# Three scatters of a second table moved between those of a first one, on GpSimd's queue

## The chip, the core and the metric

The kernel runs on one core of one Trainium2 chip, in one launch. The metric is the device time of one execution in microseconds (us); the median of several runs counts. The engines are named as in the profile: PE is TensorE (PEld is its loading of weights), DVE is VectorE, ACT is ScalarE, POOL is GpSimd and SP is SyncE. SP only starts transfers. Each engine works through its own queue in program order.

## What is computed

Three stages follow each other, for 1536 tokens of 512 features. A block-wise linear attention gives x; a dense layer follows; then a mixture of eight experts, in which each expert takes exactly 192 tokens:

```
x = attention(q, k, v, lam)                 # 1536 x 512
h = x @ w_in;  x2 = (h * clip(h + 3, 0, 6) / 6) @ w_out
logits = x2 @ w_gate                        # 8 experts
order = argsort(-logits.flatten())          # best (token, expert) pairs first
for idx in order:                           # a token goes to an expert that is not full
    tok, e = divmod(idx, 8)
    if assigned[tok] < 0 and counts[e] < 192: assigned[tok] = e; counts[e] += 1
for e in range(8):
    out[assigned == e] = relu(x2[assigned == e] @ w1[e]) @ w2[e]
```

## The kernel before

**Chunks and tables.** The tokens lie in 12 chunks of 128, numbered j from 0 to 11. The dense layer's second product gives x2 (PE, line 647, tile `x2p`). For chunks 0 to 7 one product gives all 512 features of a chunk; for chunks 8 to 11 it gives 384, and the last 128 features of these four chunks come at the very end from one product of their own (`x2_rest`, line 682, tile `x2q`), which is copied by ACT (`xq`), transposed on PE (line 691, tile `x2t`) and written by ACT and DVE (lines 694 and 695) into tile `xb`. Each value is held as two 16-bit parts, a high and a low one. So every token has a row of 768 entries in tile `xa` (384 features, two parts) and one of 288 in `xb` (128 features, two parts, and its number).

**Scatters.** While x2 is being computed, DVE, POOL and PE find the assignment in seven phases. At its end DVE writes `pos` (line 865): the place of each token in a table sorted by expert. Then POOL scatters the rows into two tables in device memory: twelve indirect transfers (one per chunk, j = 0 to 11) from `xa` into table `xsa`, here called a0 to a11, and twelve from `xb` into `xsb`, here called b0 to b11. Function `scatter` (line 875) puts a memset of one column, tile `spare`, ahead of each of them, and declares that scatters to the same table do not depend on each other.

**Experts.** The experts go in pairs. For each pair SP reads the 384 rows of the pair back with a transposing transfer: entries 0 to 767 of `xsa` (line 897) into the first six slices of tile `xs`, entries 0 to 255 of `xsb` (line 898) into the last two. Then SP loads the tokens' numbers (lines 903 and 904) and the weights (line 975). The first layer (`layer1`, line 922, tile `hp`) has four units for each expert, and each unit has two steps: one of 18 products that needs only the part from `xsa`, and one of 6 products that needs the part from `xsb` too. ACT turns a finished unit into `rr` (line 928), DVE into the two parts of `h` (lines 408 and 416), and the second layer (line 952, tile `po`) reads `h`. Its results go out by twelve more scatters.

**The order of the work.** A planner in the kernel writes out the order of each engine's queue before anything runs. Every step has booked costs, steps that it waits for and a key; among the steps that could start at the same moment on an engine the one with the smallest key comes first. A transfer is booked to end so (t is its start, the lines are 150 and 151):

```
self.dma = max(self.dma, t + 1.3) + s.nbytes * 2.78e-6
s.end = self.dma + 0.9
```

The steps named in the planner only fix the order; on the chip an instruction waits only for the data and the buffers that it really uses. In the first layer of experts 0 and 1 the 18-product steps have keys 0, 2, 4, 6 (expert 0) and 9, 11, 13, 15 (expert 1), counted from the same start, and the 6-product steps 10, 12, 14, 16 and 19, 21, 23, 25. The keys of the scatters are `GK + j` for a and `GK + 12 + j` for b.

Of the kernel before, what the change touches and what calls it, by code (L numbers as in the profile page):

```python
# [15 lines left out]
P = 128  # L16
NCH = 12
# [10 lines left out]
XB = 288  # L28
# [20 lines left out]
class Plan:  # L49
# [16 lines left out]
    def buf(self, pool, shape, dt, name):  # L66
        return Buf(self, pool, shape, dt, name)

    def add(self, eng, cost=0.0, fn=None, deps=(), bufs=(), key=0.0, reserve=0, nbytes=0):
        ways = {eng: (cost, fn)} if fn else eng  # L70
        s = Step(ways, [d for d in deps if d is not None], list(bufs), key, reserve, nbytes)
        for b in s.bufs:
            b.left += 1
        self.steps.append(s)
        return s
# [117 lines left out]
def fused_kernel(ctx, tc, raw_d, lam_d, win_d, wout_d, wg_d, w1_d, w2_d, out):  # L193
    nc = tc.nc
    te, ve, se, ge, sy = nc.tensor, nc.vector, nc.scalar, nc.gpsimd, nc.sync
# [21 lines left out]
    def C(shape, dt, name):  # L217
        return cst.tile(shape, dt, name=name)
# [411 lines left out]
    GK = -1e6  # L630

    xab, t_xa, t_xb = {}, [None] * NCH, [None] * NCH
    x_key = unit_key[4, 15] + 3
    JB = 8
    ids_in = []
    xbb = buf("B", [P, NCH, XB], F16, "xb")
# [229 lines left out]
    t_pos = add("ve", 0.9, slots, [t], [rk], GK)  # L866
# [5 lines left out]
    xsb_d = dram.tile([NCH * P, XB], F16, name="xsb")  # L872
    spare = C([P, 1], F32, "spare")

    def scatter(dst, idx, src, done):
        ge.memset(spare, 0.0)
        s = ge.indirect_dma_start(out=dst, out_offset=bass.IndirectOffsetOnAxis(ap=idx, axis=0), in_=src, in_offset=None)  # L877
        for o in done:
            tc.declare_no_dep(s.ins, o.ins, reason="distinct rows")
        done.append(s)  # L880
    sca, scb = [], []
    t_sa = [add("ge", 1.28, lambda j=j: scatter(xsa_d[:, :], pos[:, j:j + 1], xab[j // 4][:, j % 4], sca),
                [t_pos] + t_xa[j], [xab[j // 4]], GK + j, 0, 2 * P * XA) for j in range(NCH)]
    t_sb = [add("ge", 1.28, lambda j=j: scatter(xsb_d[:, :], pos[:, j:j + 1], xbb[:, j], scb),
                [t_pos] + t_xb[j] + ids_in, [xbb], GK + NCH + j, 0, 2 * P * XB) for j in range(NCH)]


    rows = C([P, NE // 2, 3], I32, "rows")
# [45 lines left out]
    def put(ps, q, z, t, key):  # L934
        os = buf("Q", [P, 512], F32, f"os{q}_{z}")
        t = add("se", c_se(512), lambda: se.activation(os[:], ps[:], AF.Copy, scale=2.0 ** -23), t, [ps, os], key)
        add("ge", 1.1, lambda: scatter(out, rows[:, q, z:z + 1], os[:], oscat), [t, t_rows], [os], key, 0, 262144)
# [104 lines left out]
```

## Time and profile before

| what | value |
|---|---|
| median of 3 runs | 514.68 us (512.02 to 515.46) |
| time of the profiled execution | 515.91 us |
| its span, first to last instruction | 514.0 us |
| mean granted PE clock | 0.986 of full |
| PE busy | 485.0 us (94%) |
| DVE busy | 397.8 us (77%) |
| ACT busy | 309.0 us (60%) |
| POOL busy | 166.6 us (32%) |

The span is what the trace covers; the 1.9 us between it and the time of that execution lie around it. Busy times are sums over the whole span; what one stage is worth is read from that stage.

### The profile page before, as it was taken

To read this page: it belongs to the slowest core of one execution; us is meant where nothing else is said; L and a number is where in the kernel's file an instruction comes from. 1 tells how busy PE (TensorE), PEld (TensorE's weight loads), DVE (VectorE), ACT (ScalarE), POOL (GpSimd) and SP (SyncE) were. 2 spreads that over 40 slices of the span, in tenths; PEclk is the share of its full clock that TensorE was granted. 3 is DMA by queue.
4 is the path that set the end of the run, shared out by engine and by line. 5 is a ranking of instruction groups with operands and counts; after the bars stand their busy time and mean duration, and the time that the engine had idled before them with its cause. 6 is when DMAs were issued, how large, how long until landed. Compare 5 with 4: busy or idle time off the path is not lost.

```text
span 514.0 us, 10307 instructions
## 1 busy us (share of the span) xinstructions
PE 485.0 (94%) x4241; PEld 296.7 (58%) x4243; DVE 397.8 (77%) x707; ACT 309.0 (60%) x486; POOL 166.6 (32%) x174
## 2 busy tenths in 40 slices
PE   7687998999999999999999999999969999999995
PEld 3476444688785444534434443556459676776762
DVE  7689999988688877589899889877524878889620
ACT  1476959764556664377669558745423767687510
POOL 2013343120222220167347436618860312223211
PEclk9889999999999999999999999999979999999999
DMA  7999326220264550000000000667368999995011
GB/s 224 400 416 412 148 83 246 84 42 2 83 246 91 97 94 8 2 1 1 1 1 2 1 1 7 240 246 240 132 149 261 327 400 356 360 354 215 1 42 41
DMA packets 44910, 77.86 MB, mean 151 GB/s; under 512 B 33080, under 2 KB 34112, under 8 KB 38720
## 3 DMA queue, kind: packets, MB, share of 16 engines
q1 hardware_dynamic: 42752, 70.82, 41.0%
q0 software_dynamic: 2112, 6.39, 3.3%
q8 instruction: 33, 0.54, 0.4%
q14 instruction: 13, 0.11, 0.1%
HBM read 63.46 MB, written 6.40 MB: 136 GB/s over the span
## 4 chain that ended last, share of the span: by engine, by line
DVE 38%; issue 22%; PE 18%; POOL 8%; ACT 8%; DMA 5%; POOLq 0%; SPq 0%; DVEq 0%; ACTq 0%
PE x2p L647 9%; DVE G L809 7%; DVE r L536 4%; DVE G L800 3%; DVE g L416 3%; POOL w L410 3%; POOL out L877 2%; ACT kd L439 2%; DVE sm L458 2%; ACT g L406 2%; DVE eq L782 2%; PE h L221 2%; DVE wid L391 2%; PE cp L828 2%; PE h L223 2%
## 5 line engine op out<-in xcount | busy, mean ns | idle before, releaser
L647 PE MATMUL x2p<-wo,g 128*128 128x512 f16 (+1 forms) x576 | 124.6, 362 | 0.0
L221 PE MATMUL h<-xT,wi 128*128 128x256 f16 (+2 forms) x304 | 90.8, 306 | 2.8 <-DVE r L536 2.8
L222 PE MATMUL h<-xT,wi 128*128 128x256 f16 (+2 forms) x304 | 90.7, 306 | 0.0
L223 PE MATMUL h<-xT,wi 128*128 128x256 f16 (+2 forms) x304 | 90.6, 306 | 0.0
L647 PEld LDWEIGHTS <-g 128*128 128x128 f16 x576 | 52.5, 99 | 55.6 <-issue 10.5
L775 POOL TENSOR_SCALAR eq<-mrow,m 128x128 bf16<-128x128 f32 x56 | 56.7, 1030 | 84.6 <-DVE on L748 52.1
L416 DVE SCALAR_TENSOR_TENSOR w<-ws,w 128x1024 f16<-128x1024 f32 x58 | 71.4, 1276 | 5.8 <-ACT w L406 5.8
L922 PE MATMUL hp<-xs,w 128*128 128x192 f16 x768 | 67.4, 251 | 3.8 <-DMA xs<-xsa 3.8
L922 PEld LDWEIGHTS <-w 128*128 128x128 f16 x768 | 65.1, 100 | 7.6 <-issue 5.2
L952 PE MATMUL po<-w,h 128*64 128x512 f16 (+1 forms) x384 | 64.1, 380 | 0.1
L406 ACT ACTIVATE w<-ws 128x1024 f16<-128x1024 f32 x64 | 63.9, 1048 | 0.1
L809 DVE TENSOR_SCALAR G<-mrow,m 128x1408 bf16<-128x1408 f32 (+10 forms) x77 | 52.0, 706 | 0.0
L385 POOL TENSOR_SCALAR wod<-wod 128x1024 f32<-128x1024 f32 x8 | 22.5, 2818 | 89.3 <-ACT wod L383 75.5
L406 ACT ACTIVATE g<-r 128x512 f16<-128x512 f32 (+1 forms) x52 | 30.8, 595 | 30.5 <-DVE r L536 29.6
L952 PEld LDWEIGHTS <-h 128*64 128x64 f16 (+1 forms) x384 | 29.0, 104 | 31.8 <-issue 1.7
L416 DVE SCALAR_TENSOR_TENSOR g<-r,g 128x512 f16<-128x512 f32 (+1 forms) x52 | 34.3, 662 | 11.4 <-ACT g L406 11.0
L536 DVE SCALAR_TENSOR_TENSOR r<-r,h 128x512 f32<-128x512 f32 (+1 forms) x52 | 33.1, 639 | 10.1 <-ACT r L535 9.8
L535 ACT ACTIVATE r<-h,c 128x512 f32<-128x512 f32 (+1 forms) x52 | 33.4, 644 | 10.9 <-PE h L223 10.8
L803 ACT ACTIVATE G<-mrow,m 128x1536 bf16<-128x1536 f32 (+3 forms) x28 | 39.4, 1407 | 0.8
L222 PEld LDWEIGHTS <-wi 128*128 128x128 f16 x304 | 30.6, 101 | 15.9 <-issue 3.2
L928 ACT ACTIVATE rr<-hp 128x384 f32<-128x384 f32 x32 | 15.6, 490 | 40.0 <-PE hp L922 39.8
L221 PEld LDWEIGHTS <-wi 128*128 128x128 f16 x304 | 30.5, 100 | 15.0 <-issue 1.5
(154 smaller groups left out, 693.2 us busy)
## 6 DMA issues: line engine op xcount, KB each, us to landing
ws<-w SPq DMA_DIRECT2D x32, 1024.0 KB, 9.3
raw<-raw SPq DMA_DIRECT2D x24, 512.0 KB, 10.0
wis<-w_in SPq DMA_DIRECT2D x8, 1024.0 KB, 14.1
wos<-w_out SPq DMA_DIRECT2D x8, 1024.0 KB, 7.8
tab<-tz SPq DMA_DIRECT2D x1, 512.0 KB, 6.3
wt<-wo SPq DMA_TRANSPOSE x16, 3.2
xsa<-xa,pos POOLq DMA_INDIRECT x12, 4.9
xsb<-xb,pos POOLq DMA_INDIRECT x12, 2.7
```

Of the source, the lines that this page charges most:

```text
L221: te.matmul(ps, lh, rh, start=start, stop=False)
L222: te.matmul(ps, lh, rl, start=False, stop=False)
L223: te.matmul(ps, ll, rh, start=False, stop=stop)
L406: h = add("se", c_se(n), lambda: se.activation(dst()[0], src(), AF.Copy, scale=sc), deps, bufs, key, reserve)
L416: lo = add("ve", c_ve(n), lambda: ve.scalar_tensor_tensor(dst()[1], src(), sc, dst()[0], op0=OP.mult, op1=OP.subtract), [h], bufs, key)
L536: t = add("ve", c_ve(nf * T), lambda: ve.scalar_tensor_tensor(r[:], r[:], 6.0 * 2.0 ** -11, ps[:], op0=OP.min, op1=OP.mult), [t], [ps, r], ...
L647: te.matmul(ps[:], gsl(y, fc, j), w[:, z, fc % 4, d0:d1], start=(fc + y + z == 0), stop=(fc == 15 and y == 1))
L775: t_eq.append(add("ge", 1.06, lambda i=i, eq=eqs[0], mrow=mrow: ge.tensor_scalar(eq[:, i], mrow[:, P * i:P * i + P], m[:, i:i + 1], None, ...
L803: se.activation(G[:, z, 0:o], mrow[:, 0:o], AF.Sign, scale=-1.0, bias=m[:, i:i + 1])
L809: ve.tensor_scalar(G[:, z, o:], mrow[:, o:], m[:, i:i + 1], None, op0=OP.is_le)
L922: te.matmul(ps[:, i], w[:, z, kk % 2, cl], x[:, 2 * kk + y, CAP * i0:CAP * i0 + CAP], start=(i + kk + y + z == 0), stop=(i == 1 and kk == ...
L952: te.matmul(o, h1[e][:, y, k, cl], w2[e, fh][0][:, zz, f], start=(k + y + zz == 0), stop=(k == 7 and y == 1))
```

## The change

A list `last_to` remembers which table the scatter before went to, and the memset is put ahead of a scatter only if that was the same table. The scatters b0, b1 and b2 get keys that put them behind a2, a5 and a8 and name these as steps to wait for in the planner; b3 to b11 name a11. The scatters of the results use the same function, so the first of them loses its memset as well.

```
+    last_to = []
+
     def scatter(dst, idx, src, done):
-        ge.memset(spare, 0.0)
+        if last_to[-1:] == [id(done)]:
+            ge.memset(spare, 0.0)
+        last_to.append(id(done))
...
     t_sb = [add("ge", 1.28, lambda j=j: scatter(xsb_d[:, :], pos[:, j:j + 1], xbb[:, j], scb),
-                [t_pos] + t_xb[j] + ids_in, [xbb], GK + NCH + j, 0, 2 * P * XB) for j in range(NCH)]
+                [t_pos] + t_xb[j] + ids_in + ([t_sa[3 * j + 2]] if j < 3 else t_sa[-1:]), [xbb], GK + (3 * j + 2.5 if j < 3 else NCH + j), 0, 2 * P * XB)
+            for j in range(NCH)]
```

## Rows read from the trace of the kernel before

**Rows 1.** PE's part of the timeline: start, us, line, operation, tile, count.

```profile
373.77 0.65 PE L691 MATMUL x2t<-ident,xq 128*128 128x128 f32 x4 [0.69 <-ACT xq L686]
378.26 18.37 PE L922 MATMUL hp<-xs,w 128*128 128x192 f16 x192 [3.84 <-DMA xs<-xsa]
396.77 10.52 PE L952 MATMUL po<-w,h 128*128 128x512 f16 x48
407.13 4.12 PE L922 MATMUL hp<-xs,w 128*128 128x192 f16 x48
...
420.67 8.09 PE L922 MATMUL hp<-xs,w 128*128 128x192 f16 x96
...
492.27 15.82 PE L952 MATMUL po<-w,h 128*128 128x512 f16 x96
```

**Rows 2.** Single microseconds: busy by engine, then granted PE clock, DMA share, GB/s.

```profile
376.00:377.00 1.00, 0.00 (x0) 0.00 (x0) 0.96 (x1) 0.95 (x2) 0.82 (x1) 0.68 1.20 328
...
382.00:383.00 1.00, 1.00 (x8) 0.92 (x7) 0.00 (x0) 0.00 (x0) 0.00 (x0) 0.50 0.21 74
...
384.00:385.00 1.00, 1.00 (x16) 1.00 (x13) 0.00 (x0) 0.00 (x0) 0.00 (x0) 1.00 0.32 50
```

**Rows 3.** SP's part of the timeline, from the first transposing transfer on.

```profile
372.47 5.84 SPq L897 DMA_TRANSPOSE xs<-xsa  x2
383.20 1.21 SPq L898 DMA_TRANSPOSE xs<-xsb  x1
...
388.01 1.50 SPq L975 DMA_DIRECT2D ws<-w  x3
```

**Rows 4.** POOL's part of the timeline: some of the 24 scatters and a memset.

```profile
346.56 1.92 POOL L877 DMA_INDIRECT xsa<-xa,pos  x1 [11.10 <-DVE pos L865]
348.49 0.12 POOL L876 MEMSET spare<- 128x1 f32 x1
348.78 0.96 POOL L877 DMA_INDIRECT xsa<-xa,pos  x1 [0.18 <-issue]
...
366.59 1.96 POOL L877 DMA_INDIRECT xsb<-xb,pos  x1 [0.19 <-issue]
...
368.86 1.97 POOL L877 DMA_INDIRECT xsa<-xa,pos  x1 [0.19 <-DVE w L416]
...
374.92 0.96 POOL L877 DMA_INDIRECT xsb<-xb,pos  x1 [0.19 <-issue]
...
376.18 1.91 POOL L877 DMA_INDIRECT xsb<-xb,pos  x1 [0.19 <-issue]
...
380.91 0.96 POOL L877 DMA_INDIRECT xsb<-xb,pos  x1 [0.19 <-issue]
```

**Rows 5.** DVE's part of the timeline.

```profile
363.28 0.56 DVE L662 SCALAR_TENSOR_TENSOR xa<-x2p,xa 128x384 f16<-128x384 f32 x1 [4.50 <-ACT xa L661]
364.23 6.90 DVE L416 SCALAR_TENSOR_TENSOR w<-ws,w 128x1024 f16<-128x1024 f32 x6 [0.39 <-ACT w L406]
...
375.09 0.69 DVE L695 TENSOR_TENSOR xb<-x2t,xb 128x512 f16<-128x512 f32 x1 [3.96 <-ACT xb L694]
376.04 2.36 DVE L416 SCALAR_TENSOR_TENSOR w<-ws,w 128x1024 f16<-128x1024 f32 x2 [0.25 <-ACT w L406]
...
392.24 0.36 DVE L408 TENSOR_SCALAR h<-rr 128x384 f16<-128x384 f32 x1 [13.84 <-ACT rr L928]
...
393.11 0.35 DVE L408 TENSOR_SCALAR h<-rr 128x384 f16<-128x384 f32 x1
```

**Rows 6.** Landing time of the first transfer of line 898, issued at 383.2 us.

```profile
DMA to landing us min/median/max: 4.9/4.9/4.9
```

**Rows 7.** Landing times of the scatters, the window 345 to 383 us.

```profile
DMA to landing us min/median/max: 2.3/3.6/7.4
```

**Rows 8.** ACT's part of the timeline: the first layer's units.

```profile
391.72 1.48 ACT L928 ACTIVATE rr<-hp 128x384 f32<-128x384 f32 x3 [14.77 <-PE hp L922]
394.69 2.47 ACT L928 ACTIVATE rr<-hp 128x384 f32<-128x384 f32 x5 [1.49 <-PE hp L922]
```

## Prediction

> **What bounds the kernel now.** I read the busy shares first, then PE's timeline, then the wait at its one gap, and from there back along SP, POOL and DVE. PE is what the whole span hangs on (485.0 of 514.0 us busy), so an edit to POOL's queue pays only where PE waits for it. While the scatters begin, PE still computes x2 without a break. It ends that work with the last transposes at 373.77 + 0.65 = 374.42, then stands still for 3.84 us until the first rows read back from the first table land, at 378.26 [rows 1]. From there to the last product, 492.27 + 15.82 = 508.09, its timeline has no further gap. What PE saves between 374.4 and 396.8 can thus be carried to the end.
>
> The gap has a price behind it as well. The granted clock falls to 0.50 of full in it (2.4 to 1.2 GHz), stays there until 383 and is 1.00 from 384 [rows 2]. A first-layer block at full clock takes 8.09 us for 96 products, 0.0843 us each; the 192 after the gap took 18.37 us where two such blocks take 16.18. So 2.2 us were lost to the clock.
>
> The wait goes back like this. The first transposing transfer starts at 372.47 and lands 5.79 us later, when PE starts [rows 1, 3]. It waited for the last scatter of the first table, a11, which POOL began at 368.86: 3.61 us from there to the transfer, 1.97 of them its own issue [rows 3, 4]. The rows that a11 sends were ready at 363.28 + 0.56 = 363.84 [rows 5]. So a11 lost 5 us in POOL's queue, where four scatters of the second table stood ahead of it. The second transfer, from the second table, starts at 383.20, lands 4.9 us later, at 388.1 [rows 3, 6], and waited for b11 (begun 380.91). b8 to b11 send rows that DVE writes at 375.09 to 375.78 [rows 5], and b8 began at 376.18, just behind.
>
> **Fewer scatters ahead of a11.** After the change eleven a and three b stand ahead of it, fourteen where it had fifteen. The fifteenth scatter began at 366.59 (b3) [rows 4], so that is when a11 would begin if nothing else changed: 2.27 us earlier, and behind its data.
>
> **Memsets left out.** Three b between the a make six places ahead of a11 where the table changes and the memset goes; a seventh is between a11 and b3. (The very first memset, and that of the first result scatter, run while POOL waits for others: nothing.) The one removed takes 0.12 us, and then 0.19 us pass before the scatter [rows 4]. A bare scatter is in no row. Its price lies between a gain of 0.31 (memset and pause both go) and a loss, x, which I bound by the landing: if a bare scatter waited for the one before it to land, at 2.3 to 7.4 us [rows 7] where 1.27 pass now, x would be 1.0 to 6.1 us. The nearest row is the memset itself: I take 0.12 to 0.31 saved, since scatters already follow each other at 1.27 us without waiting for a landing. Six times that is 0.7 to 1.9 us. So a11 begins at 364.7 to 365.9, say 365.3, the transfer at 368.9, and PE can start at 374.7, practically as soon as it is free. The gap of 3.84 us shrinks to 0.3, and with it goes the reason for the slow clock.
>
> The Trainium skill, GPSIMD Engine Reference, section Instruction dispatch, says that consecutive Pool instructions don't wait for each other's completion; a core starts the next when its share is done. By that x is zero and the change can't lose on POOL; no row here shows a bare pair.
>
> **What is late next.** b3 to b7 follow a11: from 365.3 + 1.97, with five at 1.27 us and one long one, they end at about 374.8, before the rows of b8 are ready. b8 therefore still begins at about 376.1, b11 and its transfer stay where they were, and the second table lands at 388.0 rather than 388.1. Of the 192 first-layer products of experts 0 and 1, 144 need only the first table: 144 x 0.0843 = 12.1 us, from 374.7 to 386.8. Then PE waits 1.2 us for the second table, a new gap. The remaining 48 take 4.05 us: 392.05, where they now end at 396.63.
>
> This needs the planner to put all eight 18-product steps ahead of the first 6-product step. Before it did not: ACT's three units in a row, a wait of 1.49 us, then five [rows 8] fit seven long steps, three short, the eighth long (18 x 0.0843 = 1.52 us), five short, which is the order of the keys once the second table is booked. Afterwards b3 waits, in the plan, for a11's booked landing, at X. By the bookings in the code (two latencies, the 1.3 and 0.9 us of a transfer, 725,000 bytes) the long steps are then ready at X + 0.16 + 1.3 + 2.02 + 0.9 + 0.56 = X + 4.9, while b3 starts at X + 0.16, b11 eight times 1.28 later at X + 10.4, lands at X + 12.8, and its transfer, with 2.87 and latencies of 0.16 and 0.56, makes the short steps ready at X + 16.4 or later. The distance of 11.4 us is more than seven long steps (booked at 10.4), so the eighth goes ahead. On the chip b3 does not wait for a11: the tables are distinct. These bookings give only the order; no time is taken from them.
>
> **The second layer.** It needs all of expert 0's h. Before, DVE began on the first unit at 392.24, 0.7 us after that unit's products ended, and took 0.87 us for each unit [rows 5]. Now the first unit ends at 388.5, DVE begins at 389.2, has four by 392.65, and PE goes on at 392.85, after 0.8 us more of idleness. Before it went on at 396.77: **3.9 us gained**. Expert 2's products come 10.4 us later, at 403.3 (407.13 now). The loads for its weights start at 388.01 [rows 3], still behind the transfer of line 898, so they come no earlier; before, their last needed split ended near 404, behind DVE's h work, which now ends 3.5 us sooner, and ACT's and DVE's splits of the landed weights can end near 401.4. That covers it by 2 us, and the later weights are loaded into buffers that PE itself frees, so they shift with it.
>
> **Sum.** The span goes from 514.0 to 510.1, the profiled time from 515.91 to 512.0. The median shown is 1.23 below the profiled time, so it goes from 514.68 to **510.8 us**. This hardly hangs on the memsets: PE starting 1.2 us later would only fill its wait for the second table.
>
> **Rivals.**
> First, the order on PE stays at seven long steps (chance 0.1). Then PE waits from 385.3 to 388.0 and has 66 products left: it goes on at about 393.5, 3.2 us gained, or, if the clock falls in that gap, 2.2 less: 511.5 to 513.7. For it: the planner's other bookings could shift the second table; against it, the distance above comes from one chain of steps.
> Second, the clock falls in the new gap at 387 (0.1). Before, the mean of 0.68 in the microsecond from 376 [rows 2] is full speed up to 376.36 and half after it, so PE had done nothing for 1.9 us when it fell; 1.2 is under that. If it falls, 2.2 us go: 512.8.
> Third, the weights of experts 2 and 3 become late and eat part of the shift (0.1): against it the 2 us above, for it that DVE, which makes half of each split, is busy 77% of the span. 1.5 to 2.5 us gained: about 512.7.
> Fourth, slower: a bare scatter waits for the one before it. With x each, a11 moves by 6x and b8 to b11 by 7x less the 0.9 us by which b7 now ends before b8 needs the queue. The second table then sets the end, and the change turns into a loss from 7x - 0.9 = 3.9, x = 0.7 us. At x = 1.3 (landing 2.6) the loss is 4.3: 519.0; at 6.1 it would be 37.9, some 552. Against it: spaced scatters never wait for a landing, and a memset of 0.12 us is little to make that difference; for it: nothing else says why a memset of an unused column stood there. 0.1.
> That the change doesn't reach the chip (b0 to b2 are planned behind a11 after all) makes a11 earlier still and changes nothing in the sum, since the second table decides.
> In the forecast itself (0.6) one variant matters. Five of the 24 scatters took 1.9 to 2.0 us instead of 0.96, b8 among them, beside DVE's two products at 376.04 [rows 4, 5]. Were b8 short, the end would come 1 us sooner, 509.8. The Trainium skill, GPSIMD Engine Reference, section Specifications, says that POOL shares its SBUF interfaces with VectorE and contends with instructions that have two SBUF inputs; those of line 416 are such, and b3, a11 and b8 agree. By it b8 stays long, as it is released by the same DVE work.
>
> **How the numbers follow.** The likeliest case gives 510.8, with its variant and a spread of runs of about 1 us 508.8 to 511.8; the first three rivals reach to 514. So 508.8 to 514.2, leaving out the fourth and a little beside. About 1% (5.1 us) is what a measurement of this kernel can tell from no change. Faster by more needs 509.5 or less, the variant with a favourable median: 0.18. Slower by over 1%: most of the fourth rival, 0.08. The rest, 0.74, within.
>
> **What would show it.** In the changed profile: a11 begun at 365 to 366; the first transfer at about 369; the first layer beginning by 375, at full clock; PE's timeline with a wait of about 1 us before 388 whose releaser is the second table; eight units of `rr` in one run; the second layer from about 393. Wrong it would be if bare scatters stand over 1.3 us apart, if the transfer from the second table starts later than 383.2, if the clock falls at 387, or if PE waits for weights near 403.

## The result and the profile after

The changed kernel takes 508.68 us (median of 11 runs, 507.6 to 511.18) where the one before takes 514.68: a ratio of 0.9893, 95% interval 0.987 to 0.9916. By the ratio that is 5.5 us (509.2), by the medians 6.0. The median lies 0.1 us under the range of the prediction and 2.1 under its number; the 509.2 us of the ratio lie inside the range. Of the three chances the one for faster by over 1%, 0.18, is the one that came about by a hair: 1.07%, with an interval that reaches to either side of 1%.

The profiled execution has a span of 506.3 us. It had reached the first scatter, a0, 1.9 us sooner than the one before (344.67 against 346.56 [rows 4]), ahead of all that the change touches, and the last transposes as much sooner (371.88 against 373.77 [rows 1]); that part is not the change's. The changed kernel run again had the transposes at 371.08, the same order with all memsets at 374.48: this differs from execution to execution. I therefore count from the start of the transposes. PE's timeline, columns as in [rows 1]:

```profile
371.88 0.66 PE L691 MATMUL x2t<-ident,xq 128*128 128x128 f32 x4 [0.69 <-ACT xq L686]
372.38 12.04 PE L928 MATMUL hp<-xs,w 128*128 128x192 f16 x144
384.74 4.12 PE L928 MATMUL hp<-xs,w 128*128 128x192 f16 x48 [0.32 <-DMA xs<-xsb]
389.01 10.52 PE L958 MATMUL po<-w,h 128*128 128x512 f16 x48
...
484.51 15.82 PE L958 MATMUL po<-w,h 128*128 128x512 f16 x96
```

The gap of 3.84 us is gone. All 144 products that need only the first table run at once (12.04 us); then PE waits 0.32 us, and the releaser is now the second table. From the transposes to the second layer it takes 17.13 us, where it took 396.77 - 373.77 = 23.00: 5.87 us. From there to the end of the span it is 117.3 us in both (506.3 - 389.01 and 514.0 - 396.77), so in this pair of traces the whole of it arrives.

SP's timeline, which answers to [rows 3]; the transfer from the second table is line 904 (898 before):

```profile
366.05 5.39 SPq L903 DMA_TRANSPOSE xs<-xsa  x2
381.71 1.21 SPq L904 DMA_TRANSPOSE xs<-xsb  x1
```

The instructions of that line with their landing, as in [rows 6]:

```profile
L904 SPq DMA_TRANSPOSE xs<-xsb x1: 1214/1214/1214, 381.7 to 381.7; - x1
...
DMA to landing us min/median/max: 3.0/3.0/3.0
```

POOL's timeline ([rows 4] before), from a5 on:

```profile
352.96 0.96 POOL L881 DMA_INDIRECT xsa<-xa,pos  x1 [0.19 <-issue]
354.22 0.96 POOL L881 DMA_INDIRECT xsb<-xb,pos  x1 [0.30 <-issue]
355.49 1.11 POOL L881 DMA_INDIRECT xsa<-xa,pos  x1 [0.30 <-issue]
356.60 0.12 POOL L879 MEMSET spare<- 128x1 f32 x1
356.90 0.96 POOL L881 DMA_INDIRECT xsa<-xa,pos  x1 [0.19 <-issue]
...
359.43 0.96 POOL L881 DMA_INDIRECT xsb<-xb,pos  x1 [0.30 <-issue]
360.69 0.96 POOL L881 DMA_INDIRECT xsa<-xa,pos  x1 [0.30 <-issue]
...
363.23 1.17 POOL L881 DMA_INDIRECT xsa<-xa,pos  x1 [0.19 <-issue]
364.71 1.96 POOL L881 DMA_INDIRECT xsb<-xb,pos  x1 [0.30 <-issue]
...
375.17 1.43 POOL L881 DMA_INDIRECT xsb<-xb,pos  x1 [0.19 <-issue]
...
379.43 0.96 POOL L881 DMA_INDIRECT xsb<-xb,pos  x1 [0.19 <-issue]
```

The pauses tell the two kinds apart. Ahead of a bare scatter there are 0.30 us; with a memset there are 0.12 of memset and 0.19 of pause. Either way the next scatter begins 1.26 to 1.27 us after one of 0.96. The planner put only b0 and b1 ahead of a11, behind a5 (354.22) and a8 (359.43); b2 follows a11 (364.71). Clock, ACT and DVE (columns as in [rows 2], [rows 8], [rows 5]):

```profile
376.00:377.00 1.00, 1.00 (x16) 1.00 (x14) 0.00 (x0) 0.00 (x0) 0.81 (x3) 1.00 0.08 16
...
384.00:385.00 1.00, 0.68 (x10) 0.53 (x8) 0.00 (x0) 0.00 (x0) 0.00 (x0) 1.00 0.35 20
```

```profile
385.44 3.96 ACT L934 ACTIVATE rr<-hp 128x384 f32<-128x384 f32 x8 [11.23 <-PE hp L928]
```

```profile
373.95 0.68 DVE L695 TENSOR_TENSOR xb<-x2t,xb 128x512 f16<-128x512 f32 x1
...
385.96 0.36 DVE L408 TENSOR_SCALAR h<-rr 128x384 f16<-128x384 f32 x1 [10.19 <-ACT rr L934]
...
388.94 0.56 DVE L416 SCALAR_TENSOR_TENSOR h<-rr,h 128x384 f16<-128x384 f32 x1
```

The clock stays at 1.00 through the first layer. The eight units leave PE in one run. The fourth unit of `h` ends at 388.94 + 0.56 = 389.50, half a microsecond after PE has gone on with the second layer.

### The profile page after: what moved, and what is told of

The parts are those of the page before. It is cut to its first block, busy times and chain, and to the rows that moved or that the text cites. A ratio compares the mean times of both kernels' runs of the same rounds, so it can differ in the third digit from the quotient of the medians.

```text
span 506.3 us, 10304 instructions
## 1 busy us (share of the span) xinstructions
PE 484.0 (96%) x4241; PEld 294.2 (58%) x4243; DVE 398.6 (79%) x707; ACT 309.1 (61%) x486; POOL 166.4 (33%) x167
## 4 chain that ended last, share of the span: by engine, by line
PE 35%; DVE 35%; issue 9%; ACT 8%; DMA 7%; POOL 5%; POOLq 0%; SPq 0%; DVEq 0%; ACTq 0%
PE x2p L647 11%; DVE G L809 7%; PE hp L928 6%; PE po L958 6%; DVE G L800 3%; DVE r L536 3%; DMA ws<-w 3%; DVE g L416 3%; POOL xsb L881 2%; PE h L221 2%; ACT kd L439 2%; DMA raw<-raw 2%; PE h L223 2%; PE h L222 2%; DVE sm L458 2%
## 5 line engine op out<-in xcount | busy, mean ns | idle before, releaser
L221 PE MATMUL h<-xT,wi 128*128 128x256 f16 (+2 forms) x304 | 89.4, 303 | 1.8 <-DVE r L536 1.8
L222 PE MATMUL h<-xT,wi 128*128 128x256 f16 (+2 forms) x304 | 89.3, 303 | 0.0
L223 PE MATMUL h<-xT,wi 128*128 128x256 f16 (+2 forms) x304 | 89.3, 303 | 0.0
L928 PE MATMUL hp<-xs,w 128*128 128x192 f16 x768 | 65.2, 246 | 0.3 <-DMA xs<-xsb 0.3
L928 PEld LDWEIGHTS <-w 128*128 128x128 f16 x768 | 63.2, 98 | 3.7 <-issue 2.1
L221 PEld LDWEIGHTS <-wi 128*128 128x128 f16 x304 | 30.0, 99 | 15.1 <-issue 1.6
L222 PEld LDWEIGHTS <-wi 128*128 128x128 f16 x304 | 30.1, 99 | 14.8 <-issue 2.1
L223 PEld LDWEIGHTS <-wi 128*128 128x128 f16 x304 | 30.1, 99 | 14.7
```

The lines of the kernel that those rows point to most:

```text
L221: te.matmul(ps, lh, rh, start=start, stop=False)
L222: te.matmul(ps, lh, rl, start=False, stop=False)
L223: te.matmul(ps, ll, rh, start=False, stop=stop)
L928: te.matmul(ps[:, i], w[:, z, kk % 2, cl], x[:, 2 * kk + y, CAP * i0:CAP * i0 + CAP], start=(i + kk + y + z == 0), stop=(i == 1 and kk == ...
```

## The experiments

The theory: a11 was late in POOL's queue, PE waited for it, and once it is early the second table is next, with nothing else in between. The rivals: the memsets brought part of it; the clock brought none of it; PE's order does not matter.

**The order alone.** The memset stands ahead of every scatter again.

```
-        if last_to[-1:] == [id(done)]:
-            ge.memset(spare, 0.0)
+        ge.memset(spare, 0.0)
```

> The new order of the scatters, but with the memset ahead of every one. The theory is that the order does all of it: in the changed kernel a bare scatter followed the one before it after 0.30 us, a spaced one after 0.12 + 0.19, so a memset lies inside a pause that is there anyway. It expects the same spacing of 1.26 us, a11 in the same place, no gap of PE ahead of the first layer, and 0.989 of the time before, as the changed kernel. The rival, that the memsets taken out bring part of it, expects a later a11 and a time between the two kernels.

Measured: 511.51 us, 0.9951 of the kernel before (0.9927 to 0.9976), between the two, as the rival had it. The spacing did not support the rival, though. ACT's timeline shows what was late:

```profile
365.49 0.49 ACT L661 ACTIVATE xa<-x2p 128x384 f16<-128x384 f32 x1 [9.02 <-PE x2q L682]
```

And POOL's:

```profile
366.85 0.96 POOL L880 DMA_INDIRECT xsa<-xa,pos  x1 [2.82 <-DVE xa L662]
```

The products that this ACT instruction reads had ended at 361.9; a11 waited for its rows. PE then waited 1.66 us for the first table, and its clock fell as it went on (columns as in [rows 2]):

```profile
375.22 9.05 PE L927 MATMUL hp<-xs,w 128*128 128x192 f16 x88 [1.66 <-DMA xs<-xsa]
```

```profile
376.00:377.00 1.00, 1.00 (x9) 0.92 (x7) 0.79 (x1) 0.00 (x0) 0.81 (x1) 0.50 0.89 241
```

The 88 products took 9.05 us, 1.6 more than at full clock (88 x 0.0843 = 7.4). So the late rows cost this execution the wait and the clock. The same kernel was run once more, beside the changed one on one chip:

> The changed kernel once more, beside the next one on the same chip. Expected by both theories: 0.989 of the kernel before, as on record.

> The new order with all memsets once more. It differs from the changed kernel in nine memsets on GpSimd and in nothing else: the order on every other engine is the same. Its first run came to 0.995 of the kernel before, though the scatters stood 1.26 us apart as in the changed kernel; in its profiled execution a11 was late because its rows were, 3.6 us after the products that they come from. Theory (a memset lies inside a pause): that lateness belongs to single executions, and beside the changed kernel on one chip the two are within 0.3%. The rival (the memsets cost time after all, by another way than the spacing): 0.4 to 0.6% over the changed kernel again, with the late rows in its profile again.

The two kernels differ in seven memsets (29 in one trace, 36 in the other), not in nine. The changed kernel came to 507.98 us, 0.9888 (0.9865 to 0.9911), the order alone to 508.74 us, 0.9892 (0.9864 to 0.9919). PE's timeline of the second run of the order alone:

```profile
374.48 0.66 PE L691 MATMUL x2t<-ident,xq 128*128 128x128 f32 x4 [0.69 <-ACT xq L686]
374.97 12.04 PE L927 MATMUL hp<-xs,w 128*128 128x192 f16 x144
387.21 4.12 PE L927 MATMUL hp<-xs,w 128*128 128x192 f16 x48 [0.19 <-DMA xs<-xsb]
391.47 3.83 PE L957 MATMUL po<-w,h 128*128 128x512 f16 x17
```

391.47 - 374.48 = 16.99 us, as in the changed kernel (17.13). Side by side the order does it without the memsets; the intervals are 0.3% wide to either side, so a memset effect under some 1.5 us would not show in the times. What differed in the first run was the late rows. They are not a thing of one execution: in the traces of the memsets alone and of the work in the gap (both below), which were run on one chip with it, the same ACT instruction began 2.2 us after its products, too. These two have the old order, in which a11 stands behind four b and does not feel it. The fourth run there, with scatters that wait, has its rows in time, as all other traces have. Why ACT was late there, and whether all ten runs of the order alone were slow for it, stays open.

**The memsets alone**, in the old order.

```
+        if last_to[-1:] == [id(done)]:
+            ge.memset(spare, 0.0)
+        last_to.append(id(done))
```

> The old order of the scatters, with the memset left out wherever the table changes, which is at three places. The theory (the order does all) expects the time of the kernel before, within 0.3%, with PE's gap of 3.8 us and the slow clock after it. The rival (bare scatters are cheaper) expects a11 up to 0.9 us earlier and as much off the time.

Measured: 513.74 us, 1.0001 (0.9975 to 1.0027): no difference. In this trace PE's gap was shorter and the clock did not fall in it:

```profile
373.95 0.66 PE L691 MATMUL x2t<-ident,xq 128*128 128x128 f32 x4 [0.69 <-ACT xq L686]
377.00 16.00 PE L926 MATMUL hp<-xs,w 128*128 128x192 f16 x192 [2.39 <-DMA xs<-xsa]
```

The gap is shorter because a11 began 21.07 us after a0, where it was 22.30 before (368.86 - 346.56 [rows 4]). The bare scatters are not the reason, their spacing is the same: b2 and b3 took 0.96 us each, not 1.17 and 1.96. DVE's products of line 416 began later here, at 365.63, behind the late ACT. b3 and a11:

```profile
365.57 0.96 POOL L881 DMA_INDIRECT xsb<-xb,pos  x1 [0.19 <-issue]
366.83 1.99 POOL L881 DMA_INDIRECT xsa<-xa,pos  x1 [0.30 <-issue]
```

The 192 products took 16.00 us, not 18.37, with the order of the kernel before. So the slow clock does not belong to every execution of that order. How many of them have it, the mean clock of a run does not tell. This trace has a mean of 0.988, and its low stretches lie in the first 48 us of the span, one of them here:

```profile
40.00:44.00 4.00, 3.37 (x32) 2.33 (x32) 4.00 (x8) 1.67 (x3) 0.00 (x0) 0.58 1.03 409
```

Of the 25 runs of the kernel before that were made beside this one, 11 had a mean clock of 0.991 or 0.992 (median 512.9 us) and 5 had 0.986 (median 515.5 us): a lower mean goes with a longer time, but where the clock fell in them is not shown.

**Scatters that do wait.** No memset between scatters to the tables, and for neighbours of one table the declaration is left out that they are independent.

```
-        if last_to[-1:] == [id(done)]:
+        near = last_to[-1:] == [id(done)] and done is not oscat
+        if last_to[-1:] == [id(done)] and done is oscat:
             ge.memset(spare, 0.0)
...
-        for o in done:
+        for o in done[:-1] if near else done:
```

> The new order, no memset between the 24 scatters to the tables; where two scatters to one table now follow each other directly, the independence of the two is not declared, so that the second waits for the first to land. This prices the fourth rival of the prediction. Theory: each such pair costs its landing, 2.3 to 7 us, where 1.26 pass now. Among the pairs before a11 are some eight, so a11 comes 15 to 30 us later, PE's gap grows by as much as a11 moves, less 2 us, and the time is 3 to 6% over the changed kernel. The rival, that the wait is hidden or cheap, expects less than 1%.

Measured: 543.35 us, 1.0581 (1.0523 to 1.064), by the two ratios 7% over the changed kernel: more than expected. POOL's timeline:

```profile
369.00 0.96 POOL L882 DMA_INDIRECT xsa<-xa,pos  x1 [0.30 <-issue]
372.33 0.96 POOL L882 DMA_INDIRECT xsa<-xa,pos  x1 [2.37 <-DMA xsa<-xa,pos]
...
385.00 0.96 POOL L882 DMA_INDIRECT xsa<-xa,pos  x1 [2.35 <-issue]
```

Two neighbours of the first table stand 3.3 to 5.8 us apart, two of the second 2.5 to 4.0, where 1.26 pass otherwise. a11 comes at 385.00, 40.7 us after a0 where it was 18.6; nine pairs wait ahead of it. PE waits 14.39 us for the first table and then 10.82 for the second, which the expectation had left out. That is the size that the fourth rival of the prediction would have had; a bare pair of different tables (369.00) follows after 0.30 us. The edit takes away the memset and the declaration together, so what a bare pair of one table does whose independence is declared, no run shows.

**Work in the gap** of the kernel before, whose result nobody reads.

```
         t = add("pe", 0.44, turn, [t], [xq, pt], GK)
+        fill = buf("pC", [P, 512], F32, "fill")
+
+        def keep():
+            for _ in range(16):
+                te.matmul(fill[:], wps[:, 0:4].rearrange("p a b -> p (a b)"), wps.rearrange("p a b -> p (a b)"), start=True, stop=True)
+        add("pe", 0.4, keep, [t], [fill], GK)
```

> The kernel before, with 16 products of 512 columns more on PE, whose result nobody reads, right behind the last transposes: 3.45 us of work in the gap of 3.84 us. Theory: of the gain some 2.2 us are the clock, which fell in that gap; so the first layer still begins when the first table has landed, runs at full clock (16.2 us where it took 18.4 us), and the time is 2.2 us, 0.4%, below the kernel before. The rival, that only the gap itself counts and the slow clock would have been hidden behind the second table, expects no change in the time.

Measured: 512.88 us, 0.9983 (0.9957 to 1.0009). PE's timeline:

```profile
373.55 3.62 PE L697 MATMUL fill<-wps 128*128 128x512 f16 x16
377.00 16.00 PE L928 MATMUL hp<-xs,w 128*128 128x192 f16 x192
```

The first layer ran at full clock (16.00 us). No run of the ten has a mean clock under 0.991, where 14 of the 25 of the kernel before have: this fits work that keeps the clock in those executions that would have lost it. What that is worth the times do not settle: the interval holds no change and, just, the 0.4% expected. Nor was the fill free in this trace. The first layer waited for no table; it began as the fill ended. The transfer from the first table had started at 370.19, and in the other traces this transfer takes 4.8 to 6.3 us to land, so by that estimate the table was there at 376.5 or before, and the fill held PE up by 0.5 us or more.

**Seven b ahead of a11.**

```
-                [t_pos] + t_xb[j] + ids_in + ([t_sa[3 * j + 2]] if j < 3 else t_sa[-1:]), [xbb], GK + (3 * j + 2.5 if j < 3 else NCH + j), 0, 2 * P * XB)
+                [t_pos] + t_xb[j] + ids_in + ([t_sa[-2]] if j < 7 else t_sa[-1:]), [xbb], GK + NCH + j, 0, 2 * P * XB)
             for j in range(NCH)]
+    t_sa[-1].deps += t_sb[:7]
```

> The changed kernel, but with seven scatters of the second table ahead of the last one of the first (two in the changed kernel, four in the one before). Theory: PE waits for a11, and each b ahead of it costs one spacing. Three places more than before are 3.8 us: the first layer begins 3.8 us later than in the kernel before, measured from the last transposes, and the time is 0.7% over the kernel before. The rival, that the second table bounds that stage in any case, expects the time of the kernel before at most.

Measured: 518.29 us, 1.0073 (1.0056 to 1.0089). PE's timeline:

```profile
373.08 0.66 PE L691 MATMUL x2t<-ident,xq 128*128 128x128 f32 x4 [0.69 <-ACT xq L686]
381.21 17.86 PE L929 MATMUL hp<-xs,w 128*128 128x192 f16 x192 [7.47 <-DMA xs<-xsa]
```

The gap is 3.63 us longer than before, 3.8 were expected. Each b ahead of a11 costs its place in the queue. The clock fell here 1.1 us after PE had stopped (373.74): the mean of 0.92 is full speed up to 374.84 and half after it.

```profile
374.00:375.00 1.00, 0.00 (x0) 0.00 (x0) 0.99 (x1) 1.00 (x2) 0.76 (x1) 0.92 0.49 184
```

**None ahead of a11.**

```
-                [t_pos] + t_xb[j] + ids_in + ([t_sa[3 * j + 2]] if j < 3 else t_sa[-1:]), [xbb], GK + (3 * j + 2.5 if j < 3 else NCH + j), 0, 2 * P * XB)
+                [t_pos] + t_xb[j] + ids_in + t_sa[-1:], [xbb], GK + NCH + j, 0, 2 * P * XB)
```

> The changed kernel with no scatter of the second table ahead of a11; all twelve stand behind it. Theory: PE had no wait for the first table left in the changed kernel, so an earlier a11 gains nothing; twelve b behind a11 end later than ten did, and the second table, which PE waited for by 0.3 us, comes 0 to 2.5 us later. So 0 to 2.5 us slower than the changed kernel. The rival, that a11 is still what counts, expects it faster by up to 2.5 us.

Measured: 509.39 us, 0.9897 (0.988 to 0.9913), not to be told from the changed kernel by time. PE's timeline:

```profile
372.48 12.04 PE L928 MATMUL hp<-xs,w 128*128 128x192 f16 x144
386.10 4.12 PE L928 MATMUL hp<-xs,w 128*128 128x192 f16 x48 [1.57 <-DMA xs<-xsb]
```

The first layer begins right behind the transposes (371.99), no sooner, and the wait for the second table is 1.57 us instead of 0.32. An earlier a11 gains nothing more; the two b taken from among the a stand behind them, and in this trace the second layer begins 1.2 us later after the transposes (390.36 - 371.99 = 18.37 us, 17.13 in the changed kernel). The times do not show that 1.2 us.

**A later second table.**

```
+        if done is scb and len(done) == 8:
+            for _ in range(24):
+                ge.memset(spare, 0.0)
         last_to.append(id(done))
```

> The changed kernel with 24 more memsets of one column on GpSimd ahead of b8, the first of the four scatters whose rows come last. Theory: PE now waits for the second table (by 0.3 us), so whatever b11 is later than in the changed kernel PE waits longer, one for one: with 0.1 us each, 2.4 us less the slack that stood before b8. The wait for the second table and the time should both grow by that, 1 to 2.5 us, with 2 us more if the clock falls. The rival, that the stage has slack for the second table, expects the time of the changed kernel.

Measured: 515.01 us, 1.003 (1.0007 to 1.0053), 1.4% over the changed kernel by the ratios. PE's timeline, and the clock of two single microseconds (columns as in [rows 2]):

```profile
373.79 12.04 PE L931 MATMUL hp<-xs,w 128*128 128x192 f16 x144
389.87 5.77 PE L931 MATMUL hp<-xs,w 128*128 128x192 f16 x48 [4.04 <-DMA xs<-xsb]
...
389.00:390.00 1.00, 0.13 (x2) 0.13 (x2) 0.00 (x0) 0.00 (x0) 0.00 (x0) 1.00 0.47 57
...
391.00:392.00 1.00, 1.00 (x8) 0.95 (x7) 0.88 (x3) 0.55 (x2) 0.00 (x0) 0.50 0.31 2
```

The memsets took more than I had put (376.45 to 380.78, 4.3 us). The wait grew by 3.7 us, the 48 products took 1.65 more, in part at half clock: 5.4 us in this trace. Of the 7 us another 1.4 lie ahead of the transposes (373.30, 371.88 in the changed kernel), where the edit does nothing. The second table has no slack.

**Seven long steps first**, PE's old order.

```
-                t = add("pe", 6 * len(ks) * c_pe(CAP), mms, [t, t_xs[q][ph]] + w1[0][1] + w1[1][1],
+                t = add("pe", 6 * len(ks) * c_pe(CAP), mms, [t, t_xs[q][ph]] + w1[0][1] + w1[1][1] + ([short[0, 2]] if (e, u, ph) == (1, 3, 0) else []),
...
                 l1_first.setdefault(e, t)
+                short[e, u] = t
```

> The changed kernel with PE's order in the first layer as it was before: the last step of 18 products waits, in the planner, for the third step of 6, so seven long steps stand ahead of the first short one instead of eight. Theory: PE then comes to the second table 1.5 us sooner and waits that much longer, 1.8 us; the eighth step follows later. 1.5 us, 0.3%, over the changed kernel, and 2 us more if the clock falls in that wait. The rival, that the order of PE's steps does not matter, expects the time of the changed kernel.

Measured: 510.26 us, 0.992 (0.9903 to 0.9937), 0.3% or 1.4 us over the changed kernel by the ratios, whose intervals overlap. PE's timeline:

```profile
372.93 10.56 PE L929 MATMUL hp<-xs,w 128*128 128x192 f16 x126
385.24 5.61 PE L929 MATMUL hp<-xs,w 128*128 128x192 f16 x66 [1.75 <-DMA xs<-xsb]
```

The wait is 1.75 us, as expected (1.8), and the clock holds. From the transposes to the second layer this trace takes 390.99 - 372.42 = 18.57 us, 1.4 more than the changed kernel's.

## Why the prediction was right, and where its sum was off

The mechanism was the one forecast: PE stood still for the first table, the change ends that, the second table is next, and the planner flips PE's eighth long step ahead of the short ones. Each link has a run: seven b ahead move the gap by their places, none ahead gains nothing, the second table delayed is PE's delay, and the old order of the steps costs 1.4 us in its trace.

The sum said 3.9 us; from the transposes to the second layer 5.87 were measured. By its steps:

- **Fewer scatters ahead of a11.** It counted three b, there were two. a11 began 371.88 - 363.23 = 8.65 us ahead of the transposes, where 373.77 - 365.3 = 8.47 had been put: right by two errors that cancel, this one and the next.
- **Memsets left out.** It put 0.7 to 1.9 us; nothing of it shows (1.0001 alone; the order alone 0.9892 beside 0.9888). A bare scatter follows after 0.30 us, a spaced one after 0.31.
- **The first layer begins as soon as PE is free, at full clock.** Held: 12.04 us for 144 products, 12.1 put. That the sum hardly hangs on the memsets held for the same reason.
- **The second table at 388.0.** The mis-sized term. b8 was not just behind its rows: b2 stood behind a11 too, and three of the six scatters from b2 to b7 were long, so b8 began 3.29 us after the start of the transposes, where 2.33 had been put (376.1 - 373.77), its rows being ready (373.95 + 0.68 = 374.63). It took 1.43 us, not 1.91. The transfer started 9.83 us after the start of the transposes, 0.5 later than forecast. But it landed in 3.0 us, where the profile of before had 4.9 [rows 6]. In the changed kernel and in all ten experiments this landing takes 2.9 to 3.0 us: the one row that I had was the odd one, and since PE did not wait for that landing then, nothing in that profile showed it to be odd. Only in that trace does a packet of the instruction queue q8 (0.02 MB) move during this landing, at 385.8 to 386.0 us; that it is the cause is not shown. So PE could go on with the second table 1.4 us sooner than forecast, and waited 0.32 us, not 1.2.
- **The second layer waits 0.8 us for all of expert 0's h.** The step that failed. PE went on at 389.01, directly behind the first layer, with the fourth unit of h ending at 389.50. Its products walk through h in order and begin with the first units. The same half microsecond stands in the traces of none ahead and of both second runs (the changed kernel and the order alone). From PE's start on the second table to the second layer 389.01 - 384.74 = 4.27 us passed, where 4.85 had been put (392.85 - 388.0). That is 0.6 us more, and 3.9 + 1.4 + 0.6 = 5.9.
- **The later stages keep the shift.** Held: 117.3 us from the second layer on in both.

That the gain came out over 1% was luck as far as the forecast goes: its 0.18 rested on a short b8 and a favourable median, and it came from the landing and the second layer. b8 was short in part, 1.43 us.

Of the rivals, PE's order, weights that come late and the clock falling in the new gap did not come about. The order had been priced at 0.7 us (3.2 gained instead of 3.9) and cost 1.4 in its run: the 0.8 us of the second layer's wait, in which half of it was to hide, are not there. A fall of the clock had been put at 2.2 us and cost 1.65 ahead of 48 products. The reason given against it, that 1.2 us is under 1.9, does not hold: with seven b ahead the clock fell 1.1 us after PE had stopped. The wait that was left, 0.32 us, did not put it to the test. The slow scatter was excluded for different tables; where neighbours of one table do wait, with 2.5 to 5.8 us for a pair, the kernel is 7% slower than the changed one. The Trainium skill, GPSIMD Engine Reference, section Instruction dispatch, on Pool instructions not waiting for each other, agrees with the 0.30 us between bare scatters, where the shortest landing was 2.3 us [rows 7].

The 2.2 us of clock in the sum's account of the gap belong to the profiled execution, and so does its wait of 3.84 us. The other two traces of the old order, both with the late ACT, take 19.19 us (memsets alone) and 20.09 us (work in the gap) from the transposes to the second layer, not 23.00. The 5.87 us are thus a figure of one pair of executions; the gain of the kernel is the 5.5 us of the ratio, and how it divides between the wait and the clock is not shown.

## What to carry to other kernels

Where one queue feeds two consumers, put what the first consumer waits for ahead, and then ask which of the two is late next: here the second table landed 0.3 us after PE had run out of other work, and what it came later by, PE waited longer (4.3 us of memsets, 3.7 us of wait). A cheap instruction in a pause that is there anyway costs nothing and is worth nothing to remove. A landing time of one transfer that nobody waited for, read from one trace, is a weak term; take it from several transfers or give it a range.

## What the runs showed of the hardware that I had not expected

- Between two scatters on POOL there is a pause of 0.30 us, or a memset of 0.12 us and 0.19 us; behind a scatter of 0.96 us the spacing of 1.26 us does not change. Two scatters to one table of which the second waits for the first stood 2.5 to 5.8 us apart.
- The granted clock did not fall in waits of PE of 1.57, 1.75 and 2.39 us, and fell in those of 1.66, 3.84, 4.04 and 7.47 us; so the length of the wait does not decide alone. The time from the start of the wait to the fall was not the same: 1.1 us with seven b ahead, 1.7 in the first run of the order alone, 1.9 in the kernel before; with the late second table the clock was still full in the microsecond from 389, over 3 us after PE had stopped, and fell only after it had gone on.
- A scatter takes 0.96 us or up to 1.97. That DVE's products of line 416 beside it are the reason was only argued, and they can't be the whole of it: in the trace of the kernel before a2 (350.05) and b2 (365.12) lay wholly beside such products and took 0.96 and 1.17 us.
- The same transposing transfer landed in 2.9 to 3.0 us in eleven traces and in 4.9 us in one.
